# One masked product per head and chunk in place of a tree of seven levels, in a gated recurrence followed by a feed-forward

## The chip, the core and the metric

The kernel runs on one core of a Trainium2 chip. A core has five engines that work side by side, each through its own list of instructions in order: TensorE (PE; its weight loads are shown apart as PEld), VectorE (DVE), ScalarE (ACT), GpSimd (POOL) and SyncE (SP), which here issues every transfer. The metric is the device time of one execution in microseconds (us), as the median of several executions.

## The reference

The first half is a linear recurrence with complex gates, for 4 sequences of 768 steps with 8 heads of 48 features. For every feature a state row of 48 values is multiplied by that step's gate and gets the product of key and value added. The output of a step is the query times the real part of the state.

```
mag = sqrt(a_re*a_re + a_im*a_im);  scale = minimum(mag, 0.999) / (mag + 1e-6)
for t in range(S):
    new_re = ar * S_re - ai * S_im          # ar, ai: the gates times scale, per feature
    new_im = ar * S_im + ai * S_re
    S_re, S_im = new_re + k[t] v[t]^T, new_im
    y[t] = q[t] S_re
```

The second half is a feed-forward on the 3072 tokens of 384 values: `h = max(x @ w_in, 0)` with 2048 columns, then `(h * h) @ w_out`. The inputs of the recurrence are fp32, the two weight matrices come as doubles.

## The kernel before

The steps are cut into 24 chunks of 128, six for each sequence. Features lie on the partitions: two heads of 48 rows at partitions 0 and 64, four such pairs side by side (`NP` = 4), so that one operand of a chunk is 128 x 512.

`chunk(n)` is built as follows.

- `gates` (L201 to L227) normalises the gates with two reciprocals (L214, L220), a root and several products, on DVE and ACT.
- L280 to L287 handle a step's own term: a product on GpSimd, a sum over features on TensorE (L282), a product with v, and a product with the identity that starts the output tile y (L286).
- The loop over seven levels (L295) separates each pair s < t by the middle of one block. At each level and for each of two heads, L303 multiplies keys (stationary, 48 x 128) by half of the queries (moving, 48 x 64), for the four pairs and for the real and imaginary part; L309 on DVE multiplies by the level's mask; L312 multiplies the result by v and adds it into y.
- Between levels, `next_q` and `next_gates` (DVE) and `next_k` (GpSimd) multiply the operands by the gates of the next block size; `cmul` (L190 to L194) is their four instructions, and ACT copies the untouched half (L243, L263).
- L327 adds the query times the state before the chunk, L332 copies y into x, the tokens of the feed-forward.
- L341 to L359 make the state behind the chunk: transposes of the keys, copies by ACT, products with v (L349; here the two heads follow each other and write different halves of the partitions), a complex product and a sum on DVE, and two copies into `state_mm`.

Each fp32 product in the source is two matmul instructions in the trace: L327 stands for 20 x 4 x 2 = 160 products and has 320 instructions. The feed-forward of two chunks' tokens is `first_product` (L377, then Relu and Square on ACT at L380 and L381) and `second_product` (L388, copied at L391 and stored by L392). `fill_gaps` (L369) moves the fourth pair's rows by DMA into the unused rows of the other three. `load_w1` and `load_w2` fetch the doubles in 28 tiles, and `decode` (L140 to L154) turns each into fp32 with seven DVE instructions.

The program's order is not the order on the engines: a scheduler reorders the instructions when the program is built, by a model of their costs. It gives precedence to what stands earlier in the source and fills an engine's waits with later work that is ready. On the chip that order is fixed, engine by engine. The trace shows it: at 40.59 us DVE runs a step of the weight decode (L143) among the gate products of the first chunk.

## Time and profile before

| | |
|---|---|
| device time, median of 3 runs | 1996.36 us (1995.12 to 2004.63) |
| span of the profiled execution | 2000.0 us, 26881 instructions |
| busy: PE, DVE, ACT, POOL | 1833.4, 1282.1, 408.9, 732.6 us |
| mean granted clock of TensorE | 0.746 of full |

A line of the profile that groups instructions gives the source line, engine and operation, the tiles written and read, their shape, the count, then the busy time of the group and the mean duration of one instruction in ns, and then how long the engine was idle just before them and for whom. Matmuls overlap in the pipeline, so that the mean duration of one is longer than its share of the busy time. A line of the timeline gives the start in us, the length, engine, line and operation, and the count of like instructions merged into it. The view of stretches gives for each stretch the busy time of each engine with its count, and the clock that TensorE was granted (PEclk, 1.00 is full speed).

### The profile page before, as it was taken

To read this page: it belongs to the slowest core of one execution; us is meant where nothing else is said; L and a number is where in the kernel's file an instruction comes from. 1 tells how busy PE (TensorE), PEld (TensorE's weight loads), DVE (VectorE), ACT (ScalarE), POOL (GpSimd) and SP (SyncE) were. 2 spreads that over 40 slices of the span, in tenths; PEclk is the share of its full clock that TensorE was granted. 3 is DMA by queue.
4 is the path that set the end of the run, shared out by engine and by line. 5 is a ranking of instruction groups with operands and counts; after the bars stand their busy time and mean duration, and the time that the engine had idled before them with its cause. 6 is when DMAs were issued, how large, how long until landed. Compare 5 with 4: busy or idle time off the path is not lost.

```text
span 2000.0 us, 26881 instructions
## 1 busy us (share of the span) xinstructions
PE 1833.4 (92%) x10816; PEld 1524.8 (76%) x10816; DVE 1282.1 (64%) x2247; ACT 408.9 (20%) x698; POOL 732.6 (37%) x677
## 2 busy tenths in 40 slices
PE   5678989999988989898898998999999999999999
PEld 4667668786977879687687777868868869878786
DVE  7688976768575674757747668486586574564600
ACT  1112121331221131112113113122112211311302
POOL 4332334544353341523424334153154242441400
PEclk9999875878666685867768668586786675876869
DMA  4132210111000100101011000010010000000000
GB/s 88 38 74 72 91 41 1 27 25 34 12 13 17 26 16 9 34 5 28 11 24 24 11 25 12 13 34 13 13 34 13 12 15 13 17 10 5 1 7 12
DMA packets 20091, 48.51 MB, mean 24 GB/s; under 512 B 4480, under 2 KB 11776, under 8 KB 19968
## 3 DMA queue, kind: packets, MB, share of 16 engines
q1 hardware_dynamic: 19968, 46.81, 9.4%
q8 instruction: 85, 1.39, 0.3%
q14 instruction: 38, 0.31, 0.1%
HBM read 40.89 MB, written 4.72 MB: 23 GB/s over the span
## 4 chain that ended last, share of the span: by engine, by line
PE 66%; DVE 26%; issue 4%; POOL 2%; ACT 1%; DMA 0%; SPq 0%; DVEq 0%; ACTq 0%; POOLq 0%
PE a_ps L303 38%; PE y L312 12%; PE h_ps L377 6%; PE o_ps L388 6%; DVE q L194 2%; DVE r L220 2%; DVE q L192 2%; PE y L327 1%; DVE r L214 1%; PE tp L341 1%; PE y L286 1%; DVE g L192 1%; DVE g L225 1%; PE add L349 1%; DVE a L309 1%
## 5 line engine op out<-in xcount | busy, mean ns | idle before, releaser
L303 PE MATMUL a_ps<-q,k 48*128 48x64 f32 x4608 | 792.9, 390 | 23.4 <-DVE q L192 19.3
L303 PEld LDWEIGHTS a_ps<-q,k 48*128 48x128 f32 x4608 | 748.0, 294 | 63.4 <-issue 27.4
L309 DVE TENSOR_TENSOR a<-a_ps,mask 128x256 f32<-128x256 f32 x336 | 140.2, 422 | 575.0 <-PE a_ps L303 569.7
L377 PE MATMUL h_ps<-x,w 128*128 128x256 f32 x1152 | 294.2, 412 | 34.2 <-ACT h L380 31.8
L388 PE MATMUL o_ps<-w,h 128*128 128x384 f32 x768 | 295.9, 540 | 29.3 <-ACT o L391 27.1
L312 PE MATMUL y<-a,vt 128*48 128x64 f32 x2688 | 301.2, 297 | 16.8 <-DVE a L309 16.7
L312 PEld LDWEIGHTS y<-a,vt 128*48 128x48 f32 x2688 | 246.5, 180 | 86.1 <-DVE a L309 25.8
L377 PEld LDWEIGHTS h_ps<-x,w 128*128 128x128 f32 x1152 | 230.9, 206 | 78.4 <-ACT h L380 38.7
L388 PEld LDWEIGHTS o_ps<-w,h 128*128 128x128 f32 x768 | 155.1, 209 | 135.3 <-ACT o L391 33.6
L243 ACT COPY q<-q 128x512 f32<-128x512 f32 x164 | 103.2, 629 | 454.0 <-PE a_ps L303 262.0
L263 ACT COPY k<-k 128x512 f32<-128x512 f32 x140 | 87.4, 624 | 482.8 <-POOL k L194 361.7
L214 DVE RECIPROCAL r<-sq 128x512 f32<-128x512 f32 x24 | 80.3, 3346 | 11.7 <-ACT sq L211 11.7
L220 DVE RECIPROCAL r<-r 128x512 f32<-128x512 f32 x24 | 80.4, 3348 | 0.3
L380 ACT ACTIVATE h<-h_ps 128x512 f32<-128x512 f32 x96 | 56.9, 592 | 104.5 <-PE h_ps L377 104.4
L260 POOL TENSOR_TENSOR k<-raw,g 128x256 f32<-128x256 f32 x48 | 49.3, 1047 | 77.9 <-DVE g L225 77.9
L381 ACT ACTIVATE h<-h 128x512 f32<-128x512 f32 x96 | 60.4, 629 | 2.5
L286 PE MATMUL y<-own,ident 128*128 128x512 f32 x48 | 31.8, 752 | 31.5 <-DVE own L284 31.5
L303 PEld LDWEIGHTS a_ps<-q,raw 48*128 48x128 f32 x384 | 38.0, 199 | 27.3 <-issue 15.2
L280 POOL TENSOR_TENSOR qk<-raw 128x512 f32<-128x512 f32 x24 | 31.6, 1318 | 73.1 <-PE dot L282 67.2
L343 ACT COPY kt<-tp 128x512 f32<-128x512 f32 x40 | 23.5, 587 | 142.6 <-PE tp L341 142.5
L327 PE MATMUL y<-q,state_mm 128*128 128x128 f32 x320 | 52.0, 327 | 0.0
L327 PEld LDWEIGHTS y<-q,state_mm 128*128 128x128 f32 x320 | 48.3, 238 | 2.7
(1987 smaller groups left out, 2086.4 us busy)
## 6 DMA issues: line engine op xcount, KB each, us to landing
raw<-in_feat_dram SPq DMA_DIRECT2D x48, 288.0 KB, 4.8
raw<-in_feat_dram SPq DMA_DIRECT2D x48, 192.0 KB, 3.3
words<-in_moe_w_out_dram SPq DMA_DIRECT2D x16, 384.0 KB, 3.0
vt<-in_vtok_dram SPq DMA_DIRECT2D x24, 192.0 KB, 2.5
words<-in_moe_w_in_dram SPq DMA_DIRECT2D x24, 192.0 KB, 3.5
out_dram<-o SPq DMA_DIRECT2D x24, 192.0 KB, 1.9
words<-in_moe_w_in_dram SPq DMA_DIRECT2D x24, 64.0 KB, 3.5
x<-x SPq DMA_DIRECT2D x72, 16.0 KB, 1.8
```

What stands on the lines that cost most here:

```text
L192: eng.tensor_tensor(out=out[:, RE], in0=p_[:, RE], in1=w_[:, IM], op=ALU.add if conj else ALU.subtract)
L214: nc.vector.reciprocal(out=r, in_=y)
L220: nc.vector.reciprocal(out=r, in_=r)
L243: nc.scalar.copy(out=new_[:, :, :, 0], in_=old_[:, :, :, 0])
L263: nc.scalar.copy(out=new_[:, :, :, 1], in_=old_[:, :, :, 1])
L303: nc.tensor.matmul(ps[:, p_].rearrange("s (b m) -> s b m", m=m), lhsT=xk[rows(hh), c, cols], rhs=halves(xq[:, :, cols], m)[rows(hh), c, :, 1],
L309: nc.vector.tensor_tensor(out=a, in0=ps, in1=mask[:, l].unsqueeze(1).to_broadcast([C, NP, HALF]), op=ALU.mult)
L312: nc.tensor.matmul(y[rows(hh), p_].rearrange("e (b two m) -> e b two m", two=2, m=m)[:, :, 1], lhsT=vt[n][:, HH * p_ + hh], rhs=a[:, p_].r ...
L327: nc.tensor.matmul(y[:, p_], lhsT=s[:, c, p_].rearrange("p hh e -> p (hh e)"), rhs=xq[:, c, p_ * C:(p_ + 1) * C], start=False, stop=(c == ...
L377: nc.tensor.matmul(ps[:, j], lhsT=w1[:, g, (2 * f + j) * P:(2 * f + j + 1) * P], rhs=x_of[i][:, g], start=(g == 0), stop=(g == NG - 1))
L381: nc.scalar.activation(out=h, in_=h, func=AF.Square)
L388: nc.tensor.matmul(ps, lhsT=h_of[i][f // 2][:, f % 2, t * C:(t + 1) * C], rhs=w2[:, f], start=(f == 0), stop=(f == NFB - 1))
```

## The change

The old kernel's computation stays in the program as `general_path`, without the weight loads. In front of it stands `quotient_path`, which computes everything by another form, and a test: every partition sets `good` to 1 when the sums of the squared reciprocals of the gates' magnitudes and the running products stay within given limits. If fewer than 128 partitions are good, `general_path` runs afterwards and writes the output again.

In the new form, with P[t] the running product of the gates in the chunk, the query is multiplied by P[t] and the key is divided by P[s], so that one product of 128 keys by 128 queries for each head and pair, multiplied by one triangular mask, holds all pairs of steps. Division is by the conjugate and the squared magnitude. The magnitudes' running products come from `tensor_tensor_scan`, and the complex running product from seven steps inside blocks of 8, four doublings over blocks, and one product with the block's carry.

Work goes in 12 groups of two chunks from two sequences. The fourth pair's rows lie in the gaps of the other three from the start, so that an operand for two chunks is 128 x 768 with all partitions in use; the fourth pair's operands are moved to a tile of their own (`last`) by six small DMAs, and their end products by six more. Products of the four pairs now take the two heads in turn in the innermost loop. All input loads, weights included, still go through SP; `load` now has 34 transfers for each group. `decode`, `first_product`, `second_product` and `fill_gaps` are unchanged. `load_w1` and `load_w2` now both stand behind group 0, ahead of group 1. GpSimd only sets tiles to constants and copies a few end values.

```diff
--- before.py
+++ after.py
-def tile_gateloop__then__ffn_squared_relu_kernel(
...
+def general_path(ctx, tc, feat, vtok, w1, w2, out, n_seq):
...
+@with_exitstack
+def quotient_path(ctx, tc, feat, vtok, w_in, w_out, w1, w2, out, n_seq, good):
...
+    ops = ctx.enter_context(tc.tile_pool(name="ops", bufs=2))
...
+    pa = ctx.enter_context(tc.tile_pool(name="pa", bufs=2, space=PSUM))
+    py = ctx.enter_context(tc.tile_pool(name="py", bufs=1, space=PSUM))
+    pm = ctx.enter_context(tc.tile_pool(name="pm", bufs=2, space=PSUM))
+    ph = ctx.enter_context(tc.tile_pool(name="ph", bufs=2, space=PSUM))
+    po = ctx.enter_context(tc.tile_pool(name="po", bufs=1, space=PSUM))
...
+    groups = [[(bp * GC + b) * NCH + c for b in range(GC)]
+              for bp in range(n_seq // GC) for c in range(NCH)]
+    raw = [const.tile([P, 4, GC, NG, C], F32, name=f"raw{i}") for i in range(2)]
+    vt = [const.tile([C, HH * NP, ROWS], F32, name=f"vt{i}") for i in range(2 * GC)]
...
+    def load(gi):
+        for part in (slice(A_RE, Q), slice(Q, V)):
+            for b, n in enumerate(groups[gi]):
+                for hh in range(HH):
+                    nc.sync.dma_start(out=raw[gi % 2][rows(hh), part, b],
+                                      in_=feat[n, hh, :, part, 0:NG])
+                    rest = feat[n, hh].rearrange("(g r) x p t -> g r x p t", g=NG)
+                    for g in range(NG):
+                        nc.sync.dma_start(out=raw[gi % 2][pads(hh), part, b, g],
+                                          in_=rest[g, :, part, NG])
+        for b, n in enumerate(groups[gi]):
+            nc.sync.dma_start(out=vt[gi % 2 * GC + b][:, :, 0:D],
+                              in_=vtok[n * C:(n + 1) * C].rearrange("c (h d) -> c h d", d=D))
+    load(0)
+    load(1)
...
+    def make_operands(gi):
+        r = raw[gi % 2].rearrange("p x b g t -> p x (b g t)")
+        a = r[:, A_RE:A_IM + 1]
+        sq = nrm.tile([P, 2, E], F32, name="sq")
+        nc.scalar.activation(out=sq, in_=a, func=AF.Square)
+        u, v = sq[:, 0], sq[:, 1]
+        nc.vector.scalar_tensor_tensor(out=u, in0=u, scalar=2.0 ** -80, in1=v, op0=ALU.max,
+                                       op1=ALU.add)
+        z = nrm.tile([P, E], F32, name="z")
+        nc.scalar.activation(out=z, in_=u, func=AF.Abs_reciprocal_sqrt)
+        nc.scalar.activation(out=v, in_=z, func=AF.Square, accum_out=sums[:, gi:gi + 1])
+        tt(v, u, v, ALU.mult)
+        nc.vector.tensor_scalar(out=v, in0=v, scalar1=-0.5, scalar2=1.5, op0=ALU.mult, op1=ALU.add)
+        tt(z, z, v, ALU.mult)
+        low, high = nrm.tile([P, E], F32, name="low"), nrm.tile([P, E], F32, name="high")
+        nc.scalar.activation(out=low, in_=z, func=AF.Copy, scale=-1e-6, bias=1.0)
+        nc.scalar.activation(out=high, in_=z, func=AF.Copy, scale=1e-6, bias=1.0)
+        nc.vector.tensor_scalar(out=u, in0=z, scalar1=0.999, scalar2=1.0, op0=ALU.mult, op1=ALU.min)
+        nc.vector.scalar_tensor_tensor(out=v, in0=z, scalar=1.0 / 0.999, in1=z, op0=ALU.max,
+                                       op1=ALU.mult)
+        for x, y in ((u, low), (v, high)):
+            for s in range(SEG):
+                at = slice(s * C, (s + 1) * C)
+                nc.vector.tensor_tensor_scan(out=x[:, at], data0=x[:, at], data1=y[:, at],
+                                             initial=1.0, op0=ALU.mult, op1=ALU.mult)
+        for i, x in enumerate((u, v)):
+            nc.gpsimd.tensor_copy(out=ends[:, i, gi],
+                                  in_=x.rearrange("p (s t) -> p s t", t=C)[:, :, C - 1])
+        tt(r[:, Q], r[:, Q], u, ALU.mult)
+        tt(r[:, K], r[:, K], v, ALU.mult)
+        ab = a.rearrange("p c (n j) -> p c n j", j=L)
+        n = SEG * NB
+        for j in range(1, L):
+            x, w = ab[:, :, :, j - 1], ab[:, :, :, j]
+            pr = tmp.tile([P, 2, 2, n], F32, name="pr")
+            tt(pr, x.unsqueeze(1).to_broadcast([P, 2, 2, n]),
+               w.unsqueeze(2).to_broadcast([P, 2, 2, n]), ALU.mult)
+            tt(w[:, RE], pr[:, 0, 0], pr[:, 1, 1], ALU.subtract)
+            tt(w[:, IM], pr[:, 0, 1], pr[:, 1, 0], ALU.add)
+        total = ab[:, :, :, L - 1]
+        m = 1
+        while m < NB:
+            half = total.rearrange("p c (n two m) -> p c n two m", two=2, m=m)
+            cmul(half[:, :, :, 1], half[:, :, :, 1], spread(half[:, :, :, 0, m - 1], [n // 2 // m, m]),
+                 [n // 2 // m, m], "s")
+            m *= 2
+        nc.scalar.copy(out=carry[:, :, :, 1:],
+                       in_=total.rearrange("p c (s n) -> p c s n", n=NB)[:, :, :, 0:NB - 1])
+        inner = ab[:, :, :, 0:L - 1]
+        cmul(inner, inner, spread(carry.rearrange("p c s n -> p c (s n)"), [n, L - 1]), [n, L - 1],
+             "b")
+        qk = ops.tile([P, 4, GC, NG, C], F32, name="qk")
+        flat = qk.rearrange("p x b g t -> p x (b g t)")
+        for i, x in enumerate((Q, K)):
+            tt(flat[:, 2 * i:2 * i + 2], a, r[:, x].unsqueeze(1).to_broadcast([P, 2, E]), ALU.mult)
+        ends_of = raw[gi % 2][:, A_RE:A_IM + 1, :, :, C - 1]
+        pd = prod[gi % 2]
+        shrink = u.rearrange("p (b g t) -> p b g t", g=NG, t=C)[:, :, :, C - 1]
+        for c in (RE, IM):
+            tt(pd[:, c, :, 0:NG], ends_of[:, c], shrink, ALU.mult)
+        for hh in range(HH):
+            for g in range(NG):
+                at = slice(hh * ROWS + g * PAD, hh * ROWS + (g + 1) * PAD)
+                nc.sync.dma_start(out=last[gi % 2][at], in_=qk[pads(hh), :, :, g])
+                nc.sync.dma_start(out=pd[at, :, :, NG:NP], in_=pd[pads(hh), :, :, g:g + 1])
+        operands[gi] = qk
...
+    def chunk(gi, b):
+        n = groups[gi][b]
+        c_seq = n % NCH
+        first, final = c_seq == 0, c_seq == NCH - 1
+        qk, v = operands[gi], vt[gi % 2 * GC + b]
+        def operand(i, p_, at):
+            return last[gi % 2][at, i, b] if p_ == NG else qk[at, i, b, p_]
+        y = py.tile([P, NP, C], F32, tag="y", name="y")
+        if not first:
+            s = state_mm[b]
+            for p_ in range(NP):
+                for c in (RE, IM):
+                    nc.tensor.matmul(y[:, p_], lhsT=s[:, c, p_].rearrange("p hh e -> p (hh e)"),
+                                     rhs=operand(c, p_, slice(0, P)), start=(p_ == 0 and c == RE),
+                                     stop=False, skip_group_check=True)
+        ps = [pa.tile([C, NP, C], F32, tag="a", name="a_ps") for _ in range(HH)]
+        for p_ in range(NP):
+            for c in (RE, IM):
+                for hh in range(HH):
+                    nc.tensor.matmul(ps[hh][:, p_], lhsT=operand(2 + c, p_, rows(hh)),
+                                     rhs=operand(c, p_, rows(hh)), start=(c == RE), stop=(c == IM))
+        am = []
+        for hh in range(HH):
+            am.append(att.tile([C, NP, C], F32, name="a", bufs=3))
+            tt(am[hh], ps[hh], mask.unsqueeze(1).to_broadcast([C, NP, C]), ALU.mult)
+        for p_ in range(NP):
+            for hh in range(HH):
+                nc.tensor.matmul(y[hh * ROWS:(hh + 1) * ROWS, p_], lhsT=v[:, HH * p_ + hh],
+                                 rhs=am[hh][:, p_], start=(first and p_ == 0),
+                                 stop=(p_ == NP - 1), skip_group_check=True)
+        if b == 0:
+            x_of[gi] = ffn.tile([P, NP, TOK], F32, name="x")
+        nc.scalar.copy(out=x_of[gi][:, :, b * C:(b + 1) * C], in_=y)
+        if final:
+            return
+        for c in (RE, IM):
+            tp = pm.tile([C, NG, P], F32, tag="m", name="tp")
+            for g in range(NG):
+                nc.tensor.transpose(tp[:, g], qk[:, 2 + c, b, g], ident)
+            nc.scalar.copy(out=kt[c][:, 0:NG], in_=tp)
+            nc.scalar.copy(
+                out=kt[c][:, NG].rearrange("t (hh x) -> t hh x", hh=HH)[:, :, 0:D].rearrange(
+                    "t hh (g r) -> t hh g r", g=NG),
+                in_=tp.rearrange("t g (hh x) -> t hh g x", hh=HH)[:, :, :, D:ROWS])
+        add = pm.tile([P, 2, NP, D], F32, tag="m", name="add")
+        for c in (RE, IM):
+            for p_ in range(NP):
+                for hh in range(HH):
+                    rr = slice(hh * ROWS, (hh + 1) * ROWS)
+                    nc.tensor.matmul(add[rr, c, p_], lhsT=kt[c][:, p_, rr],
+                                     rhs=v[:, HH * p_ + hh, 0:D], start=True, stop=True)
+        new = att.tile([P, 2, NP, D], F32, name="state", bufs=4)
+        if first:
+            sum_ = add
+        else:
+            sum_ = new
+            tt(sum_, add, state[n - 1], ALU.add)
+        pd = prod[gi % 2][:, :, b]
+        w = spread(pd, [NP, D])
+        p_ = tmp.tile([P, 2, NP, D], F32, tag="tp", name="p_")
+        w_ = tmp.tile([P, 2, NP, D], F32, tag="tw", name="w_")
+        tt(p_, sum_, w[RE], ALU.mult)
+        tt(w_, sum_, w[IM], ALU.mult)
+        tt(new[:, RE], p_[:, RE], w_[:, IM], ALU.add)
+        tt(new[:, IM], p_[:, IM], w_[:, RE], ALU.subtract)
+        state[n] = new
+        for hh in range(HH):
+            nc.scalar.copy(out=state_mm[b][rows(hh), :, :, hh, 0:D], in_=new[rows(hh)])
...
+    for gi in range(NGR + 1):
+        if gi < NGR:
+            make_operands(gi)
+            for b in range(GC):
+                chunk(gi, b)
+            if gi + 2 < NGR:
+                load(gi + 2)
+            fill_gaps(gi)
+        if gi == 0:
+            for j in range(FF // 512):
+                load_w1(j)
+            for j in range(4):
+                load_w2(j)
+        if gi > 0:
+            first_product(gi - 1)
+            second_product(gi - 1)
+    for x, limit, op in ((sums, 2.0 ** 14, ALU.is_le), (ends[:, 0], 2.0 ** -20, ALU.is_ge),
+                         (ends[:, 1], 2.0 ** 60, ALU.is_le)):
+        nc.vector.tensor_scalar(out=x, in0=x, scalar1=limit, scalar2=None, op0=op)
+    least = const.tile([P, 2], F32, name="least")
+    nc.vector.tensor_reduce(out=least[:, 0:1], in_=sums, op=ALU.min, axis=mybir.AxisListType.X)
+    nc.vector.tensor_reduce(out=least[:, 1:2], in_=ends.rearrange("p i n s -> p (i n s)"),
+                            op=ALU.min, axis=mybir.AxisListType.X)
+    tt(good, least[:, 0:1], least[:, 1:2], ALU.mult)
...
+    quotient_path(tc, feat, vtok, w_in, w_out, w1, w2, out, n_seq, good)
+    count = wts.tile([1, 1], I32, name="count")
+    with tc.tile_pool(name="pc", bufs=1, space=PSUM) as pc:
+        number = pc.tile([1, 1], F32, name="number")
+        nc.tensor.matmul(number, lhsT=good, rhs=ones, start=True, stop=True)
+        nc.vector.tensor_copy(out=count, in_=number)
+    n_good = nc.values_load(count, min_val=0, max_val=P)
+    with tc.If(n_good < P):
+        general_path(tc, feat, vtok, w1, w2, out, n_seq)
```

257 lines of the change are left out of this document (172 added, 85 removed).

## Prediction

> **What bounds the kernel now.** I read the profile's page first, for the engines' shares and for the chain of work that ended last.
>
> ```profile
> span 2000.0 us, 26881 instructions
> ...
> PE 1833.4 (92%) x10816; PEld 1524.8 (76%) x10816; DVE 1282.1 (64%) x2247; ACT 408.9 (20%) x698; POOL 732.6 (37%) x677
> ...
> PE 66%; DVE 26%; issue 4%; POOL 2%; ACT 1%; DMA 0%; SPq 0%; DVEq 0%; ACTq 0%; POOLq 0%
> PE a_ps L303 38%; PE y L312 12%; PE h_ps L377 6%; PE o_ps L388 6%; DVE q L194 2%; DVE r L220 2%; DVE q L192 2%; PE y L327 1%; DVE r L214 1%; PE tp L341 1%; PE y L286 1%; DVE g L192 1%; DVE g L225 1%; PE add L349 1%; DVE a L309 1%
> ```
>
> TensorE is the bound, and half of the chain is the tree's two products, L303 and L312. The feed-forward, which stays, is 12%. Next the groups by line, with shapes kept apart, for how many instructions share that time.
>
> ```profile
> L303 PE MATMUL a_ps<-q,k 48*128 48x64 f32 x4608 | 792.9, 390 | 23.4 <-DVE q L192 19.3 <-DVE q L194 3.8
> ...
> L312 PE MATMUL y<-a,vt 128*48 128x64 f32 x2688 | 301.2, 297 | 16.8 <-DVE a L309 16.7
> L388 PE MATMUL o_ps<-w,h 128*128 128x384 f32 x768 | 295.9, 540 | 29.3 <-ACT o L391 27.1 <-DVE w L154 2.2
> L377 PE MATMUL h_ps<-x,w 128*128 128x256 f32 x1152 | 294.2, 412 | 34.2 <-ACT h L380 31.8 <-DMA x<-x 2.4
> ...
> L327 PE MATMUL y<-q,state_mm 128*128 128x128 f32 x320 | 52.0, 327 | 0.0
> ...
> L341 PE MATMUL tp<-ident,k 128*128 128x128 f32 x160 | 38.0, 366 | 1.6 <-ACT kt L343 1.6
> ...
> L349 PE MATMUL add<-vt,kt 128*64 128x48 f32 x640 | 25.4, 235 | 6.1 <-ACT kt L343 6.1
> ```
>
> One instruction of L303 takes 792.9 / 4608 = 172 ns of TensorE though it streams 64 columns; one of L327 streams 128 in 52.0 / 320 = 163 ns. So the tree pays for instructions, not for columns. The view of stretches says at what clock.
>
> ```profile
> 1905.00:1925.00 20.00, 20.00 (x127) 18.55 (x127) 2.12 (x5) 0.00 (x0) 0.00 (x0) 0.50 0.00 1
> ...
> 1945.00:1965.00 20.00, 20.00 (x78) 14.63 (x78) 0.00 (x0) 4.16 (x7) 0.00 (x0) 1.00 0.06 21
> ```
>
> The first stretch holds L303 and L312 alone, the second the feed-forward alone. TensorE is busy for all 20 us in both (second number), but is granted half clock (0.50) in the first and full clock in the second. The narrow products thus run slowly and also keep the clock down.
>
> **TensorE after the change.** Full-clock prices come from starts that follow each other in TensorE's timeline.
>
> ```profile
> 1854.80 1.50 PE L327 MATMUL y<-q,state_mm 128*128 128x128 f32 x12
> 1856.14 0.60 PE L341 MATMUL tp<-ident,k 128*128 128x128 f32 x4
> 1856.58 1.03 PE L377 MATMUL h_ps<-x,w 128*128 128x256 f32 x4
> 1857.83 1.14 PE L349 MATMUL add<-vt,kt 128*64 128x48 f32 x32 [0.23 <-ACT kt L343]
> 1858.90 3.29 PE L377 MATMUL h_ps<-x,w 128*128 128x256 f32 x14
> ```
>
> ```profile
> 1955.31 20.02 PE L377 MATMUL h_ps<-x,w 128*128 128x256 f32 x92
> 1975.17 10.48 PE L388 MATMUL o_ps<-w,h 128*128 128x384 f32 x32
> ```
>
> L327: 1.34 / 12 = 112 ns. A transpose: 0.44 / 4 = 110 ns. L349: 1.07 / 32 = 33 ns. L377: 19.86 / 92 = 216 ns. L388: 10.48 / 32 = 328 ns. The feed-forward of one group is 96 x 0.216 + 64 x 0.328 = 41.7 us and is not touched.
>
> The recurrence, in instructions (two for each fp32 product): query times state stays at 320 x 0.112 = 35.8 us; transposes fall from 160 to 120, 13.2 us; L349's stay, 640 x 0.033 = 21.1 us. L303's 4992 become 24 x 4 x 2 x 2 x 2 = 768 and L312's 2688 become 24 x 4 x 2 x 2 = 384, each with 128 columns. The own term's 96 instructions (L282, L286) go. The price of the 768 and 384 isn't in the trace. Upper end: L327's 112 ns, the same 128 columns alone on the array, so 86.0 + 43.0 us. Lower end: half of it, if the two heads, which now alternate on different rows (768) or columns (384), stream together. L349 already alternates the heads' columns and costs 33 ns, against L312's 301.2 / 2688 = 112 ns without alternation, at a mixed clock and 64 columns. I take 62 ns, near the lower end, by that row: 47.6 + 23.8 us. The recurrence is then 141.5 us, 11.8 us in a group; at the upper end 199 us, 16.6 us in a group.
>
> The Trainium skill, TensorE: Matmul & The Clock Gate, Part 3 (packing small matmuls) says that matmuls in different row groups or column groups of the array run concurrently, and that K below 128 alone saves nothing. By it the lower end holds for both products; L349's row agrees for columns, and no row here shows it for rows.
>
> A group costs TensorE 41.7 + 11.8 = 53.5 us at full clock. To this come waits: in each chunk for two masks and for two copies of the transposes. A mask covers 512 elements.
>
> ```profile
> 38.64 0.69 DVE L191 TENSOR_TENSOR w__245<-q,g 128x512 f32<-128x512 f32 x1
> 39.24 0.42 DVE L190 TENSOR_TENSOR p__259<-g 128x256 f32<-128x256 f32 x1
> 39.58 0.42 DVE L192 TENSOR_TENSOR q<-p__244,w__245 128x256 f32<-128x256 f32 x1
> ```
>
> ```profile
> L343 ACT COPY kt<-tp 128x512 f32<-128x512 f32 x40 | 23.5, 587 | 142.6 <-PE tp L341 142.5
> ```
>
> DVE starts follow 0.60 us after 512 elements and 0.34 us after 256, so an operation costs about 0.08 us and 1.02 ns for each element. Two masks are 1.2 us, a copy and a half 0.9 us, so at most 4.2 us in a group where nothing fills them, and nothing where the feed-forward of the group before does, which is ready by then. I take 3.5 us. For spells at half clock I take 2 us in a group, between 0 and the 11.8 us that the whole recurrence at half clock would add. A group: 59 us.
>
> The same page, Part 1, ties half clock to windows of about 3.4 us in which TensorE idles; by it the spells cost nothing here and the sum below is 22 us lower. The stretch at 1905 differs: busy throughout, yet at half clock.
>
> **DVE and the rest.** `make_operands` has for a group: six operations on 768 elements (5.2 us) and two more (1.7); 12 scans of 128, between 0.21 us as a plain operation and 0.34 us at twice that for each element (I take 4.1 us in all); seven steps of 384 + 96 + 96 (5.8); four doublings (2.5); the carry's product, 2 x 1344 + 2 x 672 (4.4); operands, 2 x 1536 (3.3); small ones 0.2. That is 27 us, and 5 us of waits for ACT. Masks and states add 6.4 us a group. All of it, 38 us, lies under TensorE's 59. GpSimd's 732.6 us nearly vanish, off the chain. The moves to `last` wait in SP's list behind the stores of the feed-forward before (L392), which wait for ACT; TensorE has six of eight products of the other pairs to do meanwhile, and the DMA row below gives 1.8 us for a small move. Uncovered they'd cost 2 to 3 us a group, and I count them among the waits.
>
> **The start.** Here DVE and SP bound.
>
> ```profile
> 3.06 3.57 SPq L92 DMA_DIRECT2D raw<-in_feat_dram  x8
> ```
>
> ```profile
> raw<-in_feat_dram SPq DMA_DIRECT2D x48, 288.0 KB, 4.8
> ...
> x<-x SPq DMA_DIRECT2D x72, 16.0 KB, 1.8
> ```
>
> Of decode I take the stretch from 0 to 300 us, of the instructions that touch mant, power, and the fp32 weights (in the last row TensorE's two shares stand ahead of DVE's 18.44):
>
> ```profile
> 0.00:300.00 300.00, 51.51 (x84) 0.92 0.27 67
> 0.00:300.00 300.00, 74.49 (x140) 0.92 0.27 67
> 0.00:300.00 300.00, 54.18 (x160) 31.24 (x160) 18.44 (x28) 0.92 0.27 67
> ```
>
> Decode: 51.51 + 74.49 - 18.44 (counted in both) = 107.6 us for 196 instructions. SP issues a transfer in 0.45 us, so two groups' 68 loads take 31 us and the first weights land at about 35. The first 16 loads are in by 13 us, so the first operands are ready at 13 + 32 = 45 us. From 35 us DVE has 10 us of them left, 107.6 us of decode and 33 us for group 1: 186 us if it takes them in that order without a gap; if group 1 goes first, TensorE is fed from about 110 us, with the feed-forward of group 0 trickling in. I take 165 us, nearer the late end, since decode stands ahead in the source and since group 2's 34 loads (15 us of SP) stand ahead of the later weights. By then TensorE has done group 0 but for some 12 us.
>
> **The end.**
>
> ```profile
> 1996.84 0.48 ACT L391 COPY o<-o_ps 128x384 f32<-128x384 f32 x1 [10.68 <-PE o_ps L388]
> ```
>
> From here to the end of the span are 3.2 us. The test and the jump over the second path have no row; I take 10 us, between 2 and 40.
>
> **Sum.** 165 + 12 + 11 x 59 + 13 = 839 us for a profiled execution, against 2000.0. The median before, 1996.36, is 0.2% under its profile's span; so 837 us.
>
> **Rivals.**
> - No overlap of the heads: 4.8 us more in a group, 839 + 53 = 892. For it: no row shows rows overlapping.
> - Recurrence at half clock throughout: 11.8 - 2 = 9.8 us in a group, 947; with no overlap besides, up to 1050. For it: the stretch at 1905. Against it: after the change the products stream 128 columns each, as L327 does, and the feed-forward lies between.
> - DVE sets the pace. Its strided steps or scans would have to cost double: 27 us then become 54, and with 11 us of the rest 65 us a group: 11 x 65 + 190 = 905; at the slowest product in before, below, 2.6 times, 82 us a group and 1090. It decides from some 48 us for the operands.
>
> ```profile
> L190 DVE TENSOR_TENSOR p__5946<-q,g 128x512 f32<-128x512 f32 x1 | 1.8, 1790 | 0.0
> ```
>
> - An early start: fed from 110 us, 784; with no waits 745.
> - Slower: the test fails on one partition, and `general_path` runs after the new form. It costs the old span less the decode of 107.6 us and what that held up, some 1850 us, so about 2690; at the full old span 2840. It decides at one bad partition of 128. Against it: from the reference's own inputs, no magnitude is under 0.850, so a sum over 768 is at most 1063 of 16384 allowed; the shrinking product stays over 0.956 and the growing one under 2^41.2, of 2^60 allowed.
>
> **How the numbers follow.** Forecast (780 to 890) 0.58; no overlap, near 892, 0.10; half clock 0.11; DVE 0.07; early start 0.12; second path 0.02. The range 765 to 955 leaves out most of DVE's case, the double one of half clock, and the second path. A run can tell 0.5%, 10 us, from no change; only the second path is slower, and nothing in between comes near 2000: faster 0.97, same 0.01, slower 0.02.
>
> **What would show it.** Right: about 4150 matmuls; TensorE busy 85 to 90% of the span and all but idle for the first 45 us; the two new products near 60 ns each of busy time; PEclk over 0.9 from 165 us on; DVE near 510 us, GpSimd under 30; decode over by about 165 us; the feed-forward at 500 to 530 us. Wrong: a PEclk near 0.5 in the recurrence, the new products at 110 ns, TensorE idle for DVE in each group, or lines of the old path in the trace.

## The result and the profile after

The changed kernel takes 855.96 us (median of 4 runs, 854.99 to 858.16) against 2000.49 us for the kernel before on the same chip: a ratio of 0.4287, 95% interval 0.4272 to 0.4302. The forecast was 837 us, range 765 to 955. The profiled execution has a span of 856.2 us. Its page, in the same parts as before:

```profile
span 856.2 us, 11195 instructions
...
PE 720.8 (84%) x4154; PEld 536.5 (63%) x4154; DVE 528.4 (62%) x1131; ACT 248.2 (29%) x446; POOL 33.3 (4%) x44
...
PE   0035575579399999889999999999999999999997
...
DVE  4993899989989989778977494793854002010000
...
PEclk9975677569689999989999999999999999999999
...
PE 56%; DVE 28%; SPq 7%; DMA 4%; ACT 3%; issue 2%; DVEq 0%; ACTq 0%
```

TensorE's busy time fell by 1833.4 - 720.8 = 1112.6 us, nearly all of the 1143.8 us that the span lost. But the row of PE has two parts. Up to the eleventh slice (of 21.4 us each) it is half idle and VectorE (DVE) is nearly full; behind that TensorE is full. The chain says the same: VectorE holds 28% of it. The groups by line of TensorE:

```profile
L682 PE MATMUL h_ps<-x,w 128*128 128x256 f32 x1152 | 273.8, 396 | 27.5 <-DVE w L468 26.1 <-ACT h L685 1.3
L693 PE MATMUL o_ps<-w,h 128*128 128x384 f32 x768 | 269.7, 506 | 21.3 <-DVE w L468 20.3 <-ACT o L696 1.0
L613 PE MATMUL a_ps<-qk 48*128 48x128 f32 x576 | 54.3, 300 | 44.3 <-DVE qk L498 44.3
L621 PE MATMUL y<-a,vt 128*64 128x128 f32 x384 | 40.4, 304 | 18.6 <-DVE a L498 18.4
L606 PE MATMUL y<-qk,state_mm 128*128 128x128 f32 x240 | 34.9, 293 | 13.3 <-DVE qk L498 13.2
...
L613 PE MATMUL a_ps<-last 48*128 48x128 f32 x192 | 21.4, 285 | 0.0
```

The tree's 792.9 + 301.2 us became 54.3 + 21.4 us for the masked product (L613) and 40.4 us behind it (L621). TensorE is idle for 856.2 - 720.8 = 135.4 us; 44.3 + 26.1 + 20.3 + 18.4 + 13.2 = 122.3 us of it end with VectorE: with the operands (qk), the decoded weights (w) or a mask (a). Where this lies is shown by the view of stretches (columns as in the prediction: length; PE, PEld, DVE, ACT, POOL; then the clock, DMA share, GB/s):

```profile
0.00:231.00 231.00, 111.43 (x536) 73.00 (x536) 192.31 (x423) 43.47 (x73) 16.93 (x26) 0.74 0.37 95
231.00:400.00 169.00, 160.32 (x1025) 126.41 (x1026) 145.57 (x306) 64.96 (x118) 5.64 (x8) 0.95 0.25 60
400.00:800.00 400.00, 399.09 (x2409) 302.37 (x2408) 190.33 (x403) 128.53 (x237) 10.76 (x10) 1.00 0.15 37
800.00:856.00 56.00, 49.98 (x187) 34.68 (x185) 0.15 (x1) 11.26 (x19) 0.00 (x0) 0.98 0.04 13
```

Before 231 us TensorE is idle for 119.6 us and VectorE busy for 192.3 of 231. From 400 to 800 us TensorE is busy for 399.09 of 400 us and at full clock. TensorE's timeline gives a middle group, from one end of the feed-forward to the next, and the price of the new product:

```profile
529.04 0.83 PE L606 MATMUL y<-qk,state_mm 128*128 128x128 f32 x6
529.71 0.61 PE L606 MATMUL y<-last,state_mm 128*128 128x128 f32 x4
530.25 1.61 PE L613 MATMUL a_ps<-qk 48*128 48x128 f32 x24
531.69 0.61 PE L613 MATMUL a_ps<-last 48*128 48x128 f32 x8
...
585.90 0.83 PE L606 MATMUL y<-qk,state_mm 128*128 128x128 f32 x6
```

A group takes 585.90 - 529.04 = 56.9 us, and 24 instructions of L613 take 531.69 - 530.25 = 1.44 us, 60 ns each. The start, on SyncE's list, on VectorE and on TensorE:

```profile
44.32 0.72 SPq L584 DMA_DIRECT2D last<-qk  x1
...
71.24 7.06 SPq L404 DMA_DIRECT2D vt<-in_vtok_dram  x2
78.39 3.77 SPq L674 DMA_DIRECT2D x<-x  x6
82.21 3.83 SPq L480 DMA_DIRECT2D words<-in_moe_w_in_dram  x8
```

```profile
87.90 0.43 DVE L454 TENSOR_SCALAR mant<-words 128x512 int32<-128x512 int32 x1 [10.94 <-DMA words<-in_moe_w_in_dram]
```

```profile
190.76 1.50 PE L606 MATMUL y<-qk,state_mm 128*128 128x128 f32 x12
...
217.12 1.09 PE L621 MATMUL y<-a,vt 128*64 128x128 f32 x14 [0.42 <-DVE a L498]
231.42 2.90 PE L606 MATMUL y<-qk,state_mm 128*128 128x128 f32 x12 [13.21 <-DVE qk L498]
```

The encoded weights are asked for only at 82 us: in SyncE's list they stand behind the moves to `last`, which wait for group 0's operands at 44 us, behind the 34 loads of group 2, the last two of which wait for a tile of group 0, and behind `fill_gaps`. VectorE then decodes from 88 to 181 us. Most of group 1's operands were made by 77 us; what was left of them, the scans and the last products, uses the decode's scratch tiles (`low` and `high`) and ran from 182 to 191 us. Group 1's products on TensorE start at 191 us, and at 218 us TensorE waits another 13.2 us for group 2's operands. From 231 us on it has work nearly all the time.

### The profile page after: what moved, and what is told of

Same layout as the page of the kernel before. It is cut to its first block, busy times and chain, and to the rows that moved or that the text cites. A ratio compares the mean times of both kernels' runs of the same rounds, so it can differ in the third digit from the quotient of the medians.

```text
span 856.2 us, 11195 instructions
## 1 busy us (share of the span) xinstructions
PE 720.8 (84%) x4154; PEld 536.5 (63%) x4154; DVE 528.4 (62%) x1131; ACT 248.2 (29%) x446; POOL 33.3 (4%) x44
## 4 chain that ended last, share of the span: by engine, by line
PE 56%; DVE 28%; SPq 7%; DMA 4%; ACT 3%; issue 2%; DVEq 0%; ACTq 0%
PE o_ps L693 21%; PE h_ps L682 20%; PE a_ps L613 5%; DVE raw L498 5%; PE y L621 4%; DVE pr L498 4%; PE y L606 3%; SPq L401 2%; DVE sq L541 2%; DMA words<-in_moe_w_in_dram 2%; PE add L645 2%; DVE power L466 2%; DVE qk L498 2%; DVE mant L457 1%; DVE w L468 1%
## 5 line engine op out<-in xcount | busy, mean ns | idle before, releaser
L682 PE MATMUL h_ps<-x,w 128*128 128x256 f32 x1152 | 273.8, 396 | 27.5 <-DVE w L468 26.1
L693 PE MATMUL o_ps<-w,h 128*128 128x384 f32 x768 | 269.7, 506 | 21.3 <-DVE w L468 20.3
L498 DVE TENSOR_TENSOR a<-a_ps,mask 128x512 f32<-128x512 f32 x48 | 31.4, 685 | 143.0 <-PE a_ps L613 142.8
L613 PE MATMUL a_ps<-qk 48*128 48x128 f32 x576 | 54.3, 300 | 44.3 <-DVE qk L498 44.3
L498 DVE TENSOR_TENSOR pr<-raw 128x384 f32<-128x384 f32 x84 | 72.0, 857 | 21.1 <-DMA raw<-in_feat_dram 19.3
L613 PEld LDWEIGHTS a_ps<-qk 48*128 48x128 f32 x576 | 46.0, 203 | 51.8 <-DVE qk L498 44.3
L621 PE MATMUL y<-a,vt 128*64 128x128 f32 x384 | 40.4, 304 | 18.6 <-DVE a L498 18.4
L621 PEld LDWEIGHTS y<-a,vt 128*64 128x64 f32 x384 | 28.1, 150 | 29.1 <-DVE a L498 24.0
L606 PE MATMUL y<-qk,state_mm 128*128 128x128 f32 x240 | 34.9, 293 | 13.3 <-DVE qk L498 13.2
L498 DVE TENSOR_TENSOR raw<-pr 128x96 f32<-128x96 f32 x168 | 44.8, 331 | 1.7
L498 DVE TENSOR_TENSOR qk<-raw 128x1536 f32<-128x1536 f32 x24 | 41.2, 1753 | 5.3 <-PE a_ps L613 5.2
L606 PEld LDWEIGHTS y<-qk,state_mm 128*128 128x128 f32 x240 | 32.5, 204 | 18.9 <-issue 13.4
L645 PE MATMUL add<-vt,kt 128*64 128x48 f32 x640 | 28.4, 230 | 1.6 <-ACT kt L636 1.6
```

Source lines behind the costliest of these rows:

```text
L498: nc.vector.tensor_tensor(out=out, in0=in0, in1=in1, op=op)
L606: nc.tensor.matmul(y[:, p_], lhsT=s[:, c, p_].rearrange("p hh e -> p (hh e)"), rhs=operand(c, p_, slice(0, P)), start=(p_ == 0 and c == RE ...
L613: nc.tensor.matmul(ps[hh][:, p_], lhsT=operand(2 + c, p_, rows(hh)), rhs=operand(c, p_, rows(hh)), start=(c == RE), stop=(c == IM))
L621: nc.tensor.matmul(y[hh * ROWS:(hh + 1) * ROWS, p_], lhsT=v[:, HH * p_ + hh], rhs=am[hh][:, p_], start=(first and p_ == 0), stop=(p_ == NP ...
L645: nc.tensor.matmul(add[rr, c, p_], lhsT=kt[c][:, p_, rr], rhs=v[:, HH * p_ + hh, 0:D], start=True, stop=True)
L682: nc.tensor.matmul(ps[:, j], lhsT=w1[:, g, (2 * f + j) * P:(2 * f + j + 1) * P], rhs=x_of[i][:, g], start=(g == 0), stop=(g == NG - 1))
```

## Experiments

Two questions were open: what sets the late start, and whether the prices taken for TensorE were right for the reason given. For the start, theory A says that the place of the weights' loads in SyncE's list sets it; theory B says that the sum of VectorE's work for the operands of three groups and for the decode sets it.

**Weights behind group 1's operands.** The calls of `load_w1` and `load_w2` move from behind group 0 to behind `make_operands(1)`.

```
         if gi < NGR:
             make_operands(gi)
+            if gi == 1:
+                for j in range(FF // 512):
+                    load_w1(j)
+                for j in range(4):
+                    load_w2(j)
```

> The weight loads and their decode stand behind group 1's operands in the source instead of ahead of them, nothing else is changed. Theory A (two waits make the late start: the weights' transfers stand in SP's list behind group 2's loads, and group 1's operands wait for the decode because both use the same scratch buffers): the decode still runs from about 88 to 183 us, but group 1's chunks now run beneath it and TensorE is fed without a gap from about 185 us instead of 231; 800 to 815 us. Theory B (the decode's own 95 us of DVE work is what holds the start, the order does not matter): only TensorE's gap of 13 us before group 2 goes; 840 to 856 us.

Measured: 858.56 us (856.33 to 866.33), ratio 0.4283, interval 0.4253 to 0.4312. Group 1's operands were ready at 83.5 us instead of 190.7. VectorE then made most of group 2's operands, until 110 us, waited 11 us for the products that two masks need, and ran the decode from 127 to 222 us. The loads of the words now stood behind group 1's moves to `last` as well, but that held VectorE up little, as two lines of its waits up to 240 us show:

```profile
DVE a L498 <- PE a_ps L613: 14.2, 3, 6.0
DVE mant L454 <- DMA words<-in_moe_w_in_dram: 1.6, 6, 0.3
```

(A line of this view gives who waited for whom, the sum in us, the number of waits and the longest.) Group 2's operands were ready at 231.8 us, against 232.9 us. The order of the blocks on VectorE changed and their sum hardly did.

**Words on GpSimd's queue.** The weights' loads no longer stand in SyncE's list.

```
-                nc.sync.dma_start(out=words[at].rearrange("p f w -> p (f w)"),
+                nc.gpsimd.dma_start(out=words[at].rearrange("p f w -> p (f w)"),
...
-            nc.sync.dma_start(out=words[:, 0:DM].rearrange("p m w -> p (m w)"),
+            nc.gpsimd.dma_start(out=words[:, 0:DM].rearrange("p m w -> p (m w)"),
```

> The weights' transfers are issued by GpSimd's queue instead of SP's, the order in the source is as in the changed kernel. Theory A: the first weights land within 10 us, the decode begins as soon as group 0's scratch is free, at about 25 us, and ends near 140 instead of 183; group 1 still waits for its end; 805 to 820 us. Theory B: DVE was idle for some 39 us in the first 231, of which the first 10 cannot go, so no less than 827 us.

Measured: 838.7 us (834.64 to 840.34), ratio 0.4179, interval 0.4149 to 0.421, which lies below the changed kernel's. The first tile is decoded at 33 us, the last at 161 us, and group 2's operands at 211.8 us. VectorE was idle for 24 us before that, after 39 us in the changed kernel. So the queue cost 17 us of the time, and the rest of the start stayed.

**Both together.** The weights' loads go on GpSimd's queue and stand behind group 1's operands.

> Both edits: the weights on GpSimd's queue and behind group 1's operands in the source. Theory A: group 1's operands are done by about 70 us, the decode ends near 155, group 1's chunks run beneath it, TensorE is fed from about 155 us; 765 to 785 us. Theory B: the decode's work bounds as before, no less than 825 us.

Measured: 842.07 us (839.95 to 845.16), ratio 0.4206, interval 0.4176 to 0.4237. Group 1's operands were ready at 89 us, the decode ended at 205 us, and group 2's operands came at 215.0 us. Theory A's two remedies together bring no more than the queue alone.

**A decode of two steps instead of seven.** The kernel leaves out the sign and the exponent of the weights, so that VectorE's work before group 2's operands falls by 60 us; transfers and buffers are not touched.

```
         nc.vector.tensor_scalar(out=mant, in0=high, scalar1=0xFFFFF, scalar2=0x100000,
                                 op0=ALU.bitwise_and, op1=ALU.bitwise_or)
...
+        nc.vector.scalar_tensor_tensor(out=dst, in0=low.bitcast(U32), scalar=2.0 ** -32,
                                        in1=mant, op0=ALU.mult, op1=ALU.add)
```

> The decode of the weights is cut from seven DVE instructions to two in each of the 28 tiles: sign and exponent of the weights are left out, so the feed-forward computes with other weights. Transfers, buffers and the rest are unchanged. Theory B (DVE's own work up to group 2's operands, some 206 us of it, sets when TensorE is fed): DVE work falls by 28 tiles x 2.4 us = 68 us; the transfers then pace a tile at about 3 us, so that some 20 to 50 us come off: 805 to 836 us. Theory A (order in SP's list and the shared scratch set it): the first weights still land at 88 us and the tiles still come at the transfers' pace, 845 to 856 us.

Measured: 826.51 us (824.35 to 827.66), ratio 0.413, interval 0.4118 to 0.4142. Of the 60 us only 29 reached the time. Its view of waits, VectorE up to 240 us, says where the rest went:

```profile
DVE mant L454 <- DMA words<-in_moe_w_in_dram: 25.0, 12, 3.9
DVE mant L454 <- DMA words<-in_moe_w_out_dram: 18.5, 16, 2.4
```

In the changed kernel VectorE waited 12.3 us for the first words of `w_in`; here the words, behind SyncE's list and in two buffers, hold it up in every tile, 43.5 us in all. Behind VectorE's work the loads come next.

**Two steps, and the words on GpSimd's queue.** If both are right, the two gains add.

> Leaves out the sign and exponent steps of the weights' decode (two of seven VectorE instructions are kept for each tile) and issues the loads of the encoded words on GpSimd's queue instead of SyncE's. Theory B (the start is the sum of VectorE's work for three groups' operands and the decode): VectorE has some 60 us less to do before group 2's operands than in the run with GpSimd's queue alone (838.7 us), nothing holds it up, and TensorE is fed from about 155 to 170 us: 775 to 800 us. Theory A (the order of the loads alone sets the start): the shorter decode brings no more than the 27 to 30 us that it brought by itself on top of 856 less the 17 of the queue, or less because both gains are the same one: 815 to 838 us.

Measured: 807.08 us (805.14 to 809.61), ratio 0.403, interval 0.4017 to 0.4043. That is 49 us less than the changed kernel; the two gains alone add to 17 + 29 = 46. It lies between the two expectations: VectorE still waited 22.2 us for the words of `w_out`, which theory B's figure left out, and group 2's operands came at 179.6 us.

**Two of the decode's steps on GpSimd.** This was to be a kernel that beats both: the words on GpSimd's queue, and two integer steps moved from VectorE to GpSimd.

```
-        nc.vector.tensor_scalar(out=power, in0=power, scalar1=896, scalar2=896 + 255,
+        nc.gpsimd.tensor_scalar(out=power, in0=power, scalar1=896, scalar2=896 + 255,
...
-        nc.vector.tensor_scalar(out=power, in0=power, scalar1=896, scalar2=2 ** 23,
+        nc.gpsimd.tensor_scalar(out=power, in0=power, scalar1=896, scalar2=2 ** 23,
```

> The loads of the encoded words are issued on GpSimd's queue, and two of the seven steps of each tile's decode (clamp, and subtract with scale) run on GpSimd instead of VectorE. If VectorE's sum of work sets the start, some 28 x 0.8 = 22 us of it go to GpSimd, and the time is 815 to 830 us. Rival: the decode's one set of scratch tiles makes VectorE wait for GpSimd in every tile, and GpSimd's steps take longer than VectorE's did: 838 us or more.

Measured: 908.56 us (906.84 to 910.3), ratio 0.4529, interval 0.4514 to 0.4544: the rival, and slower than the changed kernel. Its groups by line for GpSimd, and its waits:

```profile
L462 POOL TENSOR_SCALAR power<-power 128x512 int32<-128x512 int32 x12 | 33.0, 2748 | 31.6 <-DVE power L460 31.6
...
L464 POOL TENSOR_SCALAR power<-power 128x512 int32<-128x512 int32 x12 | 23.3, 1944 | 0.7
```

```profile
DVE power L466 <- POOL power L464: 82.4, 26, 4.4
```

A step of 512 words takes 2.75 and 1.94 us on GpSimd, against 0.42 and 0.43 us for the same two steps on VectorE in the changed kernel. The decode has one `power` tile, so VectorE waits behind GpSimd in 26 of 28 tiles, 82.4 us, and 12.6 us less work of its own than with the queue alone (175.1 instead of 187.7 us before group 2's operands) do not make up for that.

**Group 1's feed-forward ahead of group 2's recurrence.** With the words on GpSimd's queue, TensorE's timeline still shows the wait for group 2's operands while a whole feed-forward stands behind them:

```profile
210.28 2.90 PE L606 MATMUL y<-qk,state_mm 128*128 128x128 f32 x12 [13.22 <-DVE qk L498]
```

```
+            if gi == 1:
+                fill_gaps(gi)
             if gi + 2 < NGR:
                 load(gi + 2)
...
+        if gi == 1:
+            first_product(0)
+            second_product(0)
+            first_product(1)
+            second_product(1)
+        if gi > 2:
             first_product(gi - 1)
             second_product(gi - 1)
```

> The loads of the encoded words go on GpSimd's queue as in the run of 838.7 us, and group 1's feed-forward stands ahead of group 2's recurrence in TensorE's order, with the small moves that complete its input ahead of the next group's loads. In the run of 838.7 us TensorE waits 13.2 us at 197 us for group 2's operands while group 1's feed-forward, whose input is complete by about 203 us, stands behind them in its order; the two together then take 67 us for 55 us of work. If that order is a part of the start's price, 13 to 22 us go: 817 to 826 us. Rival: VectorE, busy over 85 percent until 350 us, then delivers the next operands late and the wait comes back one group later: 833 to 842 us.

Measured: 839.05 us (836.67 to 842.1), ratio 0.4199, interval 0.4175 to 0.4223: no change against the queue alone. The 13.2 us wait went, and others came; the waits of TensorE between 180 and 500 us:

```profile
PE y L621 <- DVE a L498: 17.3, 8, 5.0
PE h_ps L682 <- DMA x<-x: 4.5, 1, 4.5
PE o_ps L693 <- ACT o L696: 3.0, 1, 3.0
```

With the queue alone the masks (first line) cost 7.9 us in that stretch. By the stretches TensorE does 53.8 us of work between 185 and 245 us instead of 41.5, and between 245 and 450 us 185.9 instead of 198.6. So in both kernels it does 240 us of work between 185 and 450 us. The rival named the right time and the right engine, but what came late were masks and not operands: group 3's were ready earlier (241.3 us instead of 251.6). The likely reading, which no further run tests, is that the feed-forward that was moved is the work that had covered the mask waits of the recurrences behind it.

The runs on the start, by the end of VectorE's last product for group 2's operands and the rest of the span behind it:

| kernel | group 2's operands ready, us | of that VectorE busy, us | rest of the span, us |
|---|---|---|---|
| changed kernel | 232.9 | 194.2 | 623.3 |
| weights behind group 1's operands | 231.8 | 192.9 | 632.3 |
| words on GpSimd's queue | 211.8 | 187.7 | 626.7 |
| both | 215.0 | 186.8 | 624.2 |
| decode of two steps | 201.5 | 133.9 | 624.4 |
| two steps, GpSimd's queue | 179.6 | 131.5 | 623.7 |
| two steps on GpSimd | 281.8 | 175.1 | 626.7 |
| feed-forward first, GpSimd's queue | 210.9 | 187.4 | 624.0 |

The last column hardly moves while the first goes from 180 to 282 us (the 632.3 is of a profiled execution that was 8 us above its kernel's median): the start is paid one to one. Its length is VectorE's work up to there plus what VectorE waits, 39 us in the changed kernel. Theory A by itself falls: the order of the blocks brought nothing, and the queue 17 us. Less work on VectorE brought more, 29 us alone and 49 us with the queue, but never all of it, since the loads came next.

**Heads in runs: rows.** Now TensorE's prices. The masked product takes one head after the other instead of the two in turn.

```
-        for p_ in range(NP):
-            for c in (RE, IM):
-                for hh in range(HH):
+        for hh in range(HH):
+            for p_ in range(NP):
+                for c in (RE, IM):
```

> In the product of keys and queries the head is now the outermost loop, so that eight products of one head (16 instructions on the same rows of the array) follow each other, where the changed kernel lets the two heads alternate. Same instructions, other order. If two heads on different rows stream together when they alternate: an instruction goes from 63 to 112 ns, 768 x 49 ns = 38 us more, 885 to 900 us. If the product is bound by its weight loads or by the waits around it, alternation is worth little: 856 to 866 us.

Measured: 873.7 us (869.35 to 874.84), ratio 0.4354, interval 0.4322 to 0.4385. The groups of L613, and two starts in the steady part:

```profile
L613 PE MATMUL a_ps<-qk 48*128 48x128 f32 x576 | 81.4, 301 | 45.3 <-DVE qk L498 44.3 <-DVE a L498 1.0
...
L613 PE MATMUL a_ps<-last 48*128 48x128 f32 x192 | 31.6, 292 | 0.0
```

```profile
595.11 1.60 PE L613 MATMUL a_ps<-qk 48*128 48x128 f32 x12
596.55 0.27 PE L613 MATMUL a_ps<-last 48*128 48x128 f32 x1
```

Twelve take 1.44 us, 120 ns each, exactly twice the 60 ns in turn, and the busy time of L613 rises from 75.7 to 113.0 us. So the two heads do stream together when they alternate on different rows. The Trainium skill, TensorE: Matmul & The Clock Gate, Part 3, says so of row groups, and this run shows it. Of the 37.3 us, 17.7 reached the time. In part that is because TensorE has slack before 231 us, and because a longer product hides some mask waits (L621 waits 11.0 us for masks in place of 18.4); the rest was not traced.

**Heads in runs: columns.** The same for the second product.

```
-        for p_ in range(NP):
-            for hh in range(HH):
+        for hh in range(HH):
+            for p_ in range(NP):
```

> In the product with v the head is the outermost loop, so that the four pairs of one head, which write the same half of the partitions, follow each other, where the changed kernel lets the heads alternate. Same instructions, other order. If two heads on different columns stream together: an instruction goes from about 62 to 112 ns, 384 x 50 ns = 19 us of TensorE, of which, as with the rows (37 us of TensorE gave 18 us of time), about half shows: 862 to 870 us. If the masks' waits bound this product: 856 us within 3.

Measured: 857.05 us (856.82 to 857.58), ratio 0.4287, interval 0.4277 to 0.4298: the changed kernel's time. The price of an instruction does change, as the same place of both timelines shows, first in turn and then in runs:

```profile
427.45 1.09 PE L621 MATMUL y<-a,vt 128*64 128x128 f32 x14
428.46 0.71 PE L613 MATMUL a_ps<-qk 48*128 48x128 f32 x8
```

```profile
426.70 1.68 PE L621 MATMUL y<-a,vt 128*64 128x128 f32 x16 [0.21 <-DVE a L498]
428.32 0.71 PE L613 MATMUL a_ps<-qk 48*128 48x128 f32 x8
```

Fourteen take 1.01 us, 72 ns each, against sixteen in 1.62 us, 101 ns each, so that the two heads overlap in part. But L621's busy time rises only from 40.4 to 46.4 us, L613's falls from 75.7 to 69.9 us, and TensorE's as a whole stays the same, 720.9 after 720.8 us. The alternation of columns is worth nothing measurable in the time here.

**The old tree with heads in turn.** The alternation is only a part of the change; put into the kernel before, it says how much it is worth by itself.

```
-            for hh in range(HH):
...
+            for p_ in range(NP):
+                cols = slice(p_ * C, (p_ + 1) * C)
+                for c in parts:
+                    for hh in range(HH):
```

> The kernel before, with one thing of the change: in each level the two heads alternate in both products, where they follow in runs. The same number of instructions. If alternation alone makes narrow products stream together: 4992 instructions go from 167 to between 60 and 120 ns and 2688 from 112 to between 60 and 90, which takes 300 to 600 us off TensorE, of which DVE and GpSimd between the levels give back a good part: 1500 to 1800 us. If the tree is bound by the chain of DVE and GpSimd from level to level: 1900 us or more.

Measured: 1843.17 us (1839.96 to 1849.07), ratio 0.9223, interval 0.9192 to 0.9253, between the two expectations. Its two products, and a stretch that holds only them:

```profile
L303 PE MATMUL a_ps<-q,k 48*128 48x64 f32 x4608 | 678.7, 394 | 40.2 <-DVE q L192 36.8 <-DVE q L194 1.4 <-POOL k L192 1.4
...
L316 PE MATMUL y<-a,vt 128*48 128x64 f32 x2688 | 228.3, 302 | 54.3 <-DVE a L311 54.3
```

```profile
1740.00:1760.00 20.00, 20.00 (x144) 18.55 (x144) 4.45 (x10) 0.62 (x1) 0.00 (x0) 0.50 0.00 1
```

The products lose 187 us of 1094 and the kernel 8%. That is 14% of the change's gain; the other 86% needs the new form, with 1152 instructions in place of the 7296 of these two rows, and at full clock. The shares depend on the order: taken out of the changed kernel, the alternation of rows is worth 17.7 us, under 2% of the gain. In this stretch of the tree the clock is 0.50 with TensorE busy all the time, as it was without the alternation. What holds the clock down there stays open.

**Without the test.** The test on the 128 partitions and the jump over the old path are taken out.

```
-    n_good = nc.values_load(count, min_val=0, max_val=P)
-    with tc.If(n_good < P):
-        general_path(tc, feat, vtok, w1, w2, out, n_seq)
```

> The jump and the second path are left out of the program, the reductions and the count stay. If the test at the end costs what the trace shows after the last copy, 5.3 us against 3.0 in the kernel before: 852 to 855 us. If the longer program or the jump costs more, as the prediction's 10 us: 846 us or less.

Measured: 853.47 us (852.95 to 856.4), ratio 0.4272, interval 0.4259 to 0.4286. By the medians the test and the jump cost 2.5 us; the two intervals overlap, so that no more than a few us can be said.

**The second path taken.** A limit that no partition meets makes the old path run behind the new one.

```
-    for x, limit, op in ((sums, 2.0 ** 14, ALU.is_le), ...
+    for x, limit, op in ((sums, 1.0, ALU.is_le), ...
```

> The limit on the sums of the logarithms is lowered from 2 to the power 14 to 1, so that the test always fails and the second path, the tree of levels, runs after the first one. If the test and the jump are real, the time is the changed kernel's 856 us plus about the whole kernel before with its own loads and decode: 2690 to 2850 us. If the second path were dead code, the time stays at 856 us within 3.

Measured: 2788.97 us (one run), inside the first expectation. (The limit is on the sums of squared reciprocals, not of logarithms, and the second path loads its own features but uses the weights decoded before.) The test is real, and the rival on the slow side, priced at 2690 to 2840 us, would have cost that: one bad partition makes the new kernel 39% slower than the one before.

## Why the prediction was right, and where it was not

The time was 19 us above the forecast and inside its own range, 780 to 890. By its terms, on the profiled execution:

```profile
850.47 0.48 ACT L696 COPY o<-o_ps 128x384 f32<-128x384 f32 x1 [10.68 <-PE o_ps L693]
```

| term | predicted, us | measured, us |
|---|---|---|
| start | 165 + 12 = 177 | 231.4 |
| eleven groups | 11 x 59 = 649 | 850.5 - 231.4 = 619.1 |
| end | 13 | 856.2 - 850.5 = 5.7 |
| sum | 839 | 856.2 |

The start is predicted to end when TensorE has eleven groups ahead of it, and measured to end when it has eleven feed-forwards ahead. By then TensorE had also done group 1's recurrence, which the prediction counts among the eleven groups, 13 us by its prices. With that moved, the start was too short by about 41 us, the groups too long by 17 and the end by 7. That the total came out near is in this respect luck: the errors have opposite signs.

- **The start failed.** The step was "I take 165 us, nearer the late end", with "By then TensorE has done group 0 but for some 12 us". The text had 186 us for the order decode, then group 1, without a gap; the trace has 190.8. It then took a value between that and an early start, and no kernel here reached the early one. More important, it stopped at group 1's operands. TensorE had little beyond group 1's recurrence then, since the feed-forward of group 1 stands behind group 2's products in its order, and group 2's operands need another 42 us of VectorE (190.7 to 232.9; the prediction's own figure for a group was 38). Its own prices give 186 + 38 = 224 us. "All of it, 38 us, lies under TensorE's 59" holds from 231 us on and not in the start.
- **The first weights.** They were to land at about 35 us, and the first decode step started at 87.9. The prediction had counted the loads in SyncE's list and not what they wait for. By the runs with GpSimd's queue that cost 17 us, not 50, since VectorE had other work meanwhile.
- **The price of the masked product** was right, and so was the reason: 62 ns taken, 60 ns measured, 120 ns without alternation. The no-overlap rival was priced at 4.8 us a group for both products; 3.2 of them for the rows, which cost 2.2 us a group in the steady part (58.8 instead of 56.6 us, each the mean of four groups). The columns cost nothing measurable in the time, and their price in turn was 72 ns, not 62.
- **The group.** By the prediction's prices a middle group is 41.7 + 13.0 us (its 11.8 is a mean over groups with and without a state). It took 56.9 us, so waits and spells at half clock were 2.2 us and not 5.5. The waits were covered: group 3's operands were ready 17 us before TensorE used them, those of a middle group 30 us (544.3 against 574.7), and from 400 to 800 us TensorE was busy for 99.8% of the time.
- **The clock.** The rival of half clock fell: 1.00 from 400 to 800 us. The Trainium skill, TensorE: Matmul & The Clock Gate, Part 1, ties half clock to windows in which TensorE idles. The changed kernel agrees, 0.74 in the start with its gaps and 1.00 from 400 to 800 us without; the tree's stretch at 0.50 with 20.00 of 20 us busy does not.
- **VectorE's sum** was right by cancelling. 528.4 us were measured for about 510. The decode took 93 us and not 107.6; the strided steps cost about twice their price (below). The rival in which VectorE sets the pace for all groups was refuted, but until group 2's operands were ready it was true.
- **The end.** 10 us were taken for the test, between 2 and 40; it costs about 2.5.

Of the signs named, the count (4154), the idle first 45 us and the absence of the old path hold. The clock was not over 0.9 from 165 us on: its mean was 0.75 between 165 and 257 us, and 0.98 between 257 and 400 us. The two new products do not show 60 ns of busy time each but 75.7 / 768 = 99 and 40.4 / 384 = 105 ns: busy time reaches past the next start (the 24 above last 1.61 us, and 1.44 us pass to the start behind them), and part of them ran at the lower clock, so that the price shows in the starts alone. VectorE's 528.4 us are near 510; TensorE's 84% and the feed-forward's 543.5 us miss the bands of 85 to 90% and 500 to 530 us by a little, GpSimd's 33.3 us exceeds 30, and the decode's end at 181 us instead of 165 showed the failed step.

What stays open is how far the start could go. Every run that shortened it left VectorE's work for the operands as it was, and a decode spread over engines without the shared tile was not tried. The best kernel that computes everything is the one with the words on GpSimd's queue: 0.4179 of the time before, 17 us better than the change.

## What to carry to other kernels

When the bound engine's work is cut by more than half, price the start anew: add up, engine by engine, all that must pass before the bound engine has work without a gap, and follow it to the second and third round, not to the first. When experiments move the point from which that engine is fed, compare the time from there to the end: if that stays the same, the time follows the point. Moving work ahead on an engine that works in order gained nothing here; look first whether that work covers later waits.

## What the hardware showed

VectorE's fp32 steps over elements 32 bytes apart cost about twice as much for each element, from the changed kernel's groups by line:

```profile
L498 DVE TENSOR_TENSOR pr<-raw 128x384 f32<-128x384 f32 x84 | 72.0, 857 | 21.1 <-DMA raw<-in_feat_dram 19.3
L498 DVE TENSOR_TENSOR raw<-pr 128x96 f32<-128x96 f32 x168 | 44.8, 331 | 1.7
...
L541 DVE TENSOR_TENSOR_SCAN sq<-sq,low 128x128 f32<-128x128 f32 x72 | 23.9, 401 | 0.9 <-ACT low L533 0.9
...
L498 DVE TENSOR_TENSOR raw<-raw,sq 128x768 f32<-128x768 f32 x24 | 21.7, 943 | 0.0
```

The last row, contiguous, is 1.2 ns an element; the first, which reads every eighth, is 2.2 ns, where the prediction had 0.47 us for the 384. A scan of 128 elements takes 0.40 us, but the scans overlap: the first group's twelve ran from 20.72 to 24.52 us, 0.32 us from start to start, inside the 0.21 to 0.34 us that the prediction bounded. And GpSimd's two integer steps took 6.5 and 4.6 times VectorE's time for a tile of the same size (2748 against 420 ns and 1944 against 427 ns).
